# Last chain, weight loads and gate copies in another order, and sixteen spare products

## The chip, the cores and the metric

The kernel runs on one core of a Trainium2 chip. The metric is device time in microseconds of one execution, from start to end. Before the change it is 1464.82 us, the median of three runs (1464.5 to 1465.57).

## What is computed

Three layers follow one another: a global filter in the frequency domain, a soft mixture of experts, and a gated feed-forward layer.

```python
def _attn_ref(x, filt_r, filt_i):                 # x: 8 x 3072 x 256
    X = np.fft.rfft(x, axis=1)
    F = (filt_r + 1j * filt_i)[None, :, :]
    return np.fft.irfft(X * F, n=x.shape[1], axis=1)

def _moe_ref(x, phi, w1, w2):                     # 24576 tokens, 8 experts, 4 slots each
    logits = x @ phi
    d = np.exp(logits - logits.max(0, keepdims=True))
    d /= d.sum(0, keepdims=True) + 1e-09          # over all tokens
    slot_input = (d.T @ x).reshape(E, S_per_e, D)
    for e in range(E):
        h = np.maximum(slot_input[e] @ w1[e], 0.0)
        slot_out[e] = h @ w2[e]
    c = np.exp(logits - logits.max(1, keepdims=True))
    c /= c.sum(1, keepdims=True) + 1e-09          # over the 32 slots
    return c @ slot_out.reshape(n_slots, D)

def _moe2_ref(x, w_gate, w_val, w_out):           # 256 -> 1536 -> 256
    g = x @ w_gate
    return (g / (1.0 + np.exp(-g)) * (x @ w_val)) @ w_out
```

The third layer is applied to `c @ slot_out`, so `x @ w_gate` is `c @ (slot_out @ w_gate)`, a product over 32 slots only. The kernel uses that: it makes the small matrices `slot_out @ w_gate` and `slot_out @ w_val` once (the gates) and multiplies them by `c` for all tokens.

## The kernel before

The program is written in an order by hand (`manual_schedule`): each engine executes its instructions in the order in which the code issues them. Waits between engines come from the data and from memory that is used again. Tiles of closed pools give their memory to later tiles, and a later tile's first writer then waits for the last readers and writers of the earlier ones.

**Phase 1** takes the sequences through the transform in steps (`s1_chunk`, `s2_unit`, `tr_unit`), half a sequence at a time, six units a step. Behind each sequence `b` runs `chain(b, last)`, a generator of some dozen stages, most of them a group of small TensorE products and a copy to SBUF. It brings the sequence's logits back to the token domain, stores them (`lgd`), takes their maximum (`cm`, `mb`) and exponentials (`dd`), transforms these (`bd`, `dt`, `dh`) and multiplies them by the sequence's data, the `y` tiles (L482). The result `sl` is the sequence's part of the slots. `pump` advances the chains between the units. The chains of the last two sequences, `g6` and `g7` (chain 6 and the last chain), are interleaved by hand behind the last unit (L747 to L755). `combine` (L517) makes the weights by which the eight parts are added: `al` and `sm` on 32 partitions, spread to 128 by a product (`psb`, L536), and a product of each part with its weighted identity (`rb`), fourteen for the first seven parts (`pss`, L548) and two for the last (L502). The sum goes to `sp`.

**The transition** loads the second expert weights on SyncE's queue (`load_w2`, L770; the order of the loads is that of two loops), and the gate weights `wg` and `wv` (`flat_load`, L127). These tiles lie where phase 1's tiles lay, so some loads wait for phase 1's last products. It then runs the experts in two halves: `stage1` (`h`, L812), `turn` (transposes `t`, L829), `stage2` (`o`, L837; its first product reads `w2_0`). `later["first"]()` (L911) loads the first tile of mixing weights `c` from `cd` and the prepared output weights `wo`. Then come `so` and `sot`, the gate products (L872 and L883) and their split into a rounded part and a rest (`gh` and `gl`, in FP32R, each 128 x 512). Sixteen copies from SBUF to SBUF (L895) spread them over the partitions of `g4` and `v4`, eight on SyncE's queue and eight on GpSimd's. Columns 0 to 511 of the gates need no such copy.

**Phase 2** has 576 items of 512 tokens and 128 columns. For each, `gv` issues the products G and V (L988, L989), ScalarE takes the Silu (`s`, L991), VectorE multiplies (`h`, L997), `split` makes `hi` and `lo` (L1004, L1005), and `proj` issues six products `o` (L1026), three or four items behind `gv` (`lag`). In the first twelve items `load_out(i)` makes a rounded part and a rest of one chunk of `wo` on ScalarE (L977) and GpSimd (L978). The last group of twelve items is issued by `close` (L1048, L1052), with the copies and sums of its end (L1060, L1061) and four stores (L1069). The pool `kp` holds the tiles `s`, `h`, `hi`, `lo`, `ot` and `tmp`.

The order of the stages of phase 2's engines is one loop:

```python
        for i in range(len(items) + LAG):
            if i < len(items):
                ...
                gv(i)
            while todo and todo[0] <= i - lag(i):
                n = todo.pop(0)
                (close if n >= len(items) - NF else proj)(n)
            if i < len(items):
                gate(i)
            if i < NF:
                load_out(i)
            if 0 <= i - 1 < len(items):
                split(i - 1)
```

Of the kernel before, what the change touches and what calls it, by code (L numbers as in the profile page):

```python
# [20 lines left out]
NF = FF // 128  # L21
LAG = 4
EXP_AT = 17
HOLD = 9
# [55 lines left out]
def spectral_softmoe_glu_kernel(  # L80
# [56 lines left out]
    def phase1():  # L137
        with ExitStack() as c1:
# [4 lines left out]
            cvp = c1.enter_context(tc.tile_pool(name="cvp", bufs=1))  # L143
# [5 lines left out]
            ps_s1 = c1.enter_context(tc.tile_pool(name="ps_s1", bufs=1, space=PSUM))  # L149
            ps_x = c1.enter_context(tc.tile_pool(name="ps_x", bufs=2, space=PSUM))  # L150
            ps_t = c1.enter_context(tc.tile_pool(name="ps_t", bufs=1, space=PSUM))
            ps_l = c1.enter_context(tc.tile_pool(name="ps_l", bufs=1, space=PSUM))
            ps_c = c1.enter_context(tc.tile_pool(name="ps_c", bufs=1, space=PSUM))
# [154 lines left out]
            def chain(b, last):  # L308
# [3 lines left out]
                def two(late=False):  # L312
# [9 lines left out]
                    ps = ps_s1.tile([128, 1024], F32, tag="s1", name="cl")  # L322
                    return [ps[:, 0:512], ps[:, 512:1024]]

                def pair(name):
                    if b == NB - 2 and name in ("dt", "dh"):
                        t = ytp.tile([128, 768], F32, tag="yt", name=name)
                        return [t[:, 0:512], t[:, 512:768]]
# [58 lines left out]
                cm = chp.tile([128, E], F32, tag="cm", name="cm")  # L387
# [9 lines left out]
                both = bass.AP(pl[0].tensor, pl[0].offset, [list(pl[0].ap[0]), [16, E], [512, 2], [1, 16]])  # L397
                dve.tensor_reduce(out=cm, in_=both, axis=AX.XY, op=ALU.max)
                for h in range(2):
                    act.copy(lg[h], pl[h].rearrange("p (e n) -> p e n", n=16))  # L400
# [7 lines left out]
                if not last:  # L408
                    yield
                ps = small()  # L410
                pe.transpose(out=ps[0:32, 0:128], in_=cm, identity=ident)
                dve.tensor_reduce(
                    out=mb[:, b:b + 1],
                    in_=ps[0:32, 0:128].rearrange("p (g n) -> p g n", g=2)[:, :, 0:48],
# [22 lines left out]
                if last:  # L437
# [3 lines left out]
                bd = chp.tile([128, E, 32], F32, tag="lg", name="bd")  # L441
                pl = (ps_s1.tile([128, 1024], F32, tag="s1", name="cl") if last else small()).rearrange(
                    "p (g e n) -> p g e n", g=2, n=16
                )
                for h in range(2):
                    for g in range(2):
# [5 lines left out]
                        )  # L452
                for es in es2:
                    turn(bd, pl[:, :, es].rearrange("p g e n -> p e g n"), es)
                yield
                ps = two(True)
                for jj in range(NJ):
# [6 lines left out]
                    )  # L464
                dt_ = evac("dt", ps)
# [7 lines left out]
                for k in range(6):  # L473
                    pe.transpose(out=col(ps, k), in_=col(dt_, k), identity=ident)
                if last:
                    rb, pss = next(com)
                dh = evac("dh", ps)
                yield
                ps = two(True)[0] if b == NB - 2 else small()
                for k in range(6):  # L480
# [9 lines left out]
                    if k in (2, 5) and b == NB - 2:  # L490
                        yield
# [4 lines left out]
                act.copy(sl, ps[:, 0:256])  # L496
                if b < NB - 2:
                    nc.scalar.dma_start(out=sld[:, b, :], in_=sl)
                if last:
                    next(com)  # L500
                    for d_ in range(2):
                        pe.matmul(  # L502
                            out=pss[d_][:, 0:32], lhsT=sl[:, d_ * 128:(d_ + 1) * 128], rhs=rb[:, b, :],
                            start=False, stop=True,
                        )
                        (dve.tensor_copy if d_ else act.copy)(sp[:, d_, :], pss[d_][:, 0:32])
# [9 lines left out]

            def combine():  # L517
# [5 lines left out]
                beta4 = chp.tile([128, NB, 1], F32, tag="beta4", name="beta4")  # L523
                dve.tensor_reduce(out=mx, in_=mb, axis=AX.X, op=ALU.max)
                dve.tensor_scalar(al, mb, mx, None, ALU.subtract)
                act.activation(al, al, AF.Exp)
                yield
# [4 lines left out]
                dve.tensor_scalar(al, al, sm, 2.0 / SEQ, ALU.mult, ALU.mult)  # L532
                yield
                rb = chp.tile([128, NB, 32], F32, tag="t4", name="rb")
                psb = ps_t.tile([128, 512], F32, tag="T", name="psb")
                pe.matmul(out=psb[:, 0:NB], lhsT=rep4[0:32, :], rhs=al)  # L536
                dve.tensor_copy(beta4[:, :, 0], psb[:, 0:NB])
                dve.tensor_tensor(
                    out=rb,
                    in0=rep4[:, None, 0:32].to_broadcast([128, NB, 32]),  # L540
                    in1=beta4.to_broadcast([128, NB, 32]),
                    op=ALU.mult,
                )
                pss = [ps_x.tile([128, 512], F32, tag="X", name="pss") for _ in range(2)]
                yield rb, pss
                for d_ in range(2):
                    for b in range(NB - 1):
                        pe.matmul(  # L548
                            out=pss[d_][:, 0:32],
                            lhsT=slots[b // 4][:, b % 4, d_ * 128:(d_ + 1) * 128],  # L550
                            rhs=rb[:, b, :],
# [587 lines left out]
```

## Time and profile before

| what | us |
|---|---|
| median of three runs | 1464.82 (1464.5 to 1465.57) |
| the profiled execution | 1466.01 |
| its span in the trace | 1464.2 |
| phase 1 up to the last product of the last chain | about 378 |
| transition (experts, gates) up to the first output product | 378.7 to 410.8 |
| phase 2 | 410.8 to the end |
| busy: TensorE, VectorE, ScalarE, GpSimd | 1414.5, 1147.1, 905.0, 243.4 |

Times in the rows are counted from the start of the span. A span is 1.8 us shorter than its execution's own time. In phase 2 TensorE executes eight products an item without a pause; between chain 6 and the first output product the engines wait for one another, and this is the stretch that the rows below show closely.

### The profile page before, as it was taken

The numbers are of one execution on the slowest core, as the hardware profiler recorded it, in microseconds if no ns is written. First come the engines' busy times: TensorE is split into PE (matmuls) and PEld (weight loads), VectorE is DVE, ScalarE is ACT, GpSimd is POOL, SyncE is SP. The second block draws the span as 40 slices with busy tenths as digits, with TensorE's granted clock in tenths as the row PEclk, the third lists the DMA queues.
The fourth block names the chain that finished last, engine by engine and source line by source line (L and its number), as shares of the span: only waits on it lengthen the run. The fifth ranks groups of instructions, "written<-read, shape, count | busy, mean of one in ns | idle before, by whom it ended". The sixth has DMA issues, their size and how long they took to land.

```text
span 1464.2 us, 22633 instructions
## 1 busy us (share of the span) xinstructions
PE 1414.5 (97%) x8446; PEld 1101.4 (75%) x8446; DVE 1147.1 (78%) x1776; ACT 905.0 (62%) x1650; POOL 243.4 (17%) x315
## 2 busy tenths in 40 slices
PE   4899999998999999999999999999999999999998
PEld 2566666665567888888888888888888888888887
DVE  2788888877188878878887897888779878877775
ACT  2466667764266667666766666676666667666664
POOL 0466666663030000000000000000000000000000
PEclk9999999999999999999999999999999999999999
DMA  9979888978721231231131112212210320221111
GB/s 230 158 121 165 148 135 145 185 156 338 281 50 19 37 67 24 37 61 30 30 59 40 29 31 56 40 29 44 55 29 15 73 40 16 54 47 21 24 29 30
DMA packets 178077, 116.26 MB, mean 79 GB/s; under 512 B 105136, under 2 KB 161328, under 8 KB 177840
## 3 DMA queue, kind: packets, MB, share of 16 engines
q1 hardware_dynamic: 170720, 102.37, 35.6%
q10 hardware_dynamic: 6800, 11.54, 2.7%
q8 instruction: 67, 1.10, 0.3%
q0 software_dynamic: 448, 0.92, 0.2%
q14 instruction: 42, 0.34, 0.1%
HBM read 68.13 MB, written 34.60 MB: 70 GB/s over the span
## 4 chain that ended last, share of the span: by engine, by line
PE 91%; DVE 4%; ACT 2%; DMA 1%; issue 1%; POOL 1%; SPq 0%; ACTq 0%; POOLq 0%; DVEq 0%
PE o L1026 52%; PE V L989 9%; PE G L988 9%; PE X L258 5%; PE s L230 4%; PE T L283 2%; PE L L291 1%; PE c L482 1%; DMA x<-in_x_dram 1%; DVE sg L238 1%; PE o L1048 1%; PE c L364 1%; DVE P L262 1%; PE h L812 1%; PE c L447 1%
## 5 line engine op out<-in xcount | busy, mean ns | idle before, releaser
L1026 PE MATMUL o<-hi,wo 128*128 128x512 f32 x2256 | 696.3, 390 | 2.7 <-POOL wo L978 2.7
L991 ACT ACTIVATE s<-G 128x512 f32<-128x512 f32 x576 | 344.7, 598 | 331.7 <-PE G L988 327.6
L997 DVE TENSOR_TENSOR h<-V,s 128x512 f32<-128x512 f32 x576 | 393.5, 683 | 154.6 <-ACT s L991 151.8
L1026 PEld LDWEIGHTS o<-hi,wo 128*128 128x128 f32 x2256 | 424.5, 188 | 91.3 <-POOL wo L978 3.0
L1026 PE MATMUL o<-lo,wo 128*128 128x512 f32 x1128 | 439.5, 390 | 0.0
L1005 DVE TENSOR_TENSOR lo<-h,hi 128x512 fp32r<-128x512 f32 x576 | 421.5, 732 | 1.1
L1004 ACT CAST hi<-h 128x512 fp32r<-128x512 f32 x576 | 354.2, 615 | 36.4 <-DVE h L997 35.1
L1026 PEld LDWEIGHTS o<-lo,wo 128*128 128x128 f32 x1128 | 212.0, 188 | 43.9
L989 PE MATMUL V<-c,v 128*128 128x512 f32 x576 | 224.9, 390 | 1.2 <-DVE h L997 1.2
L988 PE MATMUL G<-c,g 128*128 128x512 f32 x576 | 224.7, 390 | 0.3 <-ACT s L991 0.3
L258 PEld LDWEIGHTS X<-fwd,b 128*128 128x128 f32 x768 | 95.2, 195 | 57.0 <-issue 40.3
L989 PEld LDWEIGHTS V<-c,v 128*128 128x128 f32 x576 | 108.4, 188 | 25.0 <-DVE h L997 2.7
L988 PEld LDWEIGHTS G<-c,g 128*128 128x128 f32 x576 | 108.2, 188 | 24.4 <-ACT s L991 1.1
L238 DVE STREAM_TRANSPOSE sg<-s 128x1024 f32<-128x1024 f32 x64 | 78.9, 1236 | 58.4 <-PE s L230 56.7
L258 PE MATMUL X<-fwd,b 128*128 128x128 f32 x768 | 111.6, 289 | 2.2 <-ACT b L247 1.2
L935 POOL TENSOR_TENSOR lg<-lg,mx 96x1024 f32<-96x1024 f32 x7 | 16.8, 2405 | 550.3 <-DVE mx L933 550.3
L230 PE MATMUL s<-x,csm 48*64 48x512 f32 x512 | 73.7, 632 | 18.6 <-DMA x<-in_x_dram 16.6
L247 ACT COPY b<-sg 128x768 f32<-128x768 f32 x64 | 59.0, 925 | 52.8 <-DVE sg L238 52.6
L271 POOL TENSOR_TENSOR yt<-P 128x256 f32<-128x256 f32 x96 | 70.4, 734 | 117.7 <-DVE P L262 117.2
L1031 DVE STREAM_TRANSPOSE ot<-o 128x512 f32<-128x512 f32 x94 | 65.1, 714 | 29.6 <-PE o L1026 29.6
L262 DVE TENSOR_TENSOR P<-X,ft 128x512 f32<-128x512 f32 x96 | 64.6, 672 | 12.0 <-PE X L258 11.8
L273 POOL TENSOR_TENSOR yt<-Q 128x256 f32<-128x256 f32 x95 | 69.5, 731 | 0.2
(202 smaller groups left out, 969.6 us busy)
## 6 DMA issues: line engine op xcount, KB each, us to landing
out_dram<-ot SPq DMA_DIRECT2D x192, 128.0 KB, 2.8
x<-in_x_dram SPq DMA_DIRECT2D x60, 384.0 KB, 8.2
w<-in_moe_w_dram SPq DMA_DIRECT2D x8, 1024.0 KB, 10.2
w<-in_moe_w_dram ACTq DMA_DIRECT2D x13, 512.0 KB, 6.9
c<-ch SPq DMA_DIRECT2D x42, 128.0 KB, 2.4
c<-cl SPq DMA_DIRECT2D x42, 128.0 KB, 2.4
raw<-in_moe_w_gate_dram SPq DMA_DIRECT2D x12, 256.0 KB, 5.2
raw<-in_moe_w_val_dram SPq DMA_DIRECT2D x12, 256.0 KB, 5.8
```

The source lines that it names most:

```text
L230: pe.matmul(out=ps[64 * k:64 * k + 64, 16 * r:16 * r + 16, :], lhsT=s1t_sb[64 * r:64 * r + 48, :], rhs=xt[step][64 * r:64 * r + 48, k, :, ...
L238: dve.transpose(out=sg.rearrange("p j d k -> p d j k"), in_=ps.rearrange("p n d -> p d n"))
L258: pe.matmul(out=ps[:, g].rearrange("p r m -> p (r m)"), lhsT=bb[:, j, :], rhs=fwd[:, j, :])
L262: dve.tensor_tensor(out=P, in0=ps, in1=f, op=ALU.mult)
L271: pool.tensor_tensor(out=y[:, :, 0, :], in0=P[:, :, 0, :], in1=P[:, :, 1, :], op=ALU.subtract)
L988: pe.matmul(out=pg, lhsT=g4[c][:, fs], rhs=c4[b][:, q, G, :])
L989: pe.matmul(out=pv, lhsT=v4[c][:, fs], rhs=c4[b][:, q, G, :])
L991: act.activation(s, pg, AF.Silu)
L997: dve.tensor_tensor(out=h, in0=pv, in1=s, op=ALU.mult)
L1004: act.copy(hi, h)
L1005: dve.tensor_tensor(out=lo, in0=h, in1=hi, op=ALU.subtract)
L1026: pe.matmul(out=a[h], lhsT=w[:, k, h], rhs=m, start=(f == 0 and n == 0), stop=(f == NF - 1 and n == 2), skip_group_check=True,)
```

## The change

1. **Weight loads of stage 1.** The `w1` loads are issued on SyncE's queue instead of ScalarE's, and earlier. Pools are placed so that this is possible (`cvp` on the other side, a new pool `w6`, PSUM pools in another order); three `pump(1)` fewer than ten remain, so chain 6's `dd` product comes later.
2. **The last chain.** The maximum `cm` is made in two reductions between the two copies `lg`. Chain 6's L482 products are split into pieces of eight, four, four and eight between products of the last chain. In `combine` the weights are spread before the sum of exponentials is known, VectorE adds up the parts in a running sum (`acc`) and multiplies by the last weight in `sl`; the fourteen `pss` products are gone, and the factor `sm` comes with `rb`. Seven products of 128 columns without a use (`warm`) stand in the chain.
3. **Second expert weights.** The loads come in another order, and `w2_0` lies elsewhere in SBUF (it was the first tile of the stack, and is now behind `gl`), by which all tiles between lie 8 KB lower.
4. **Gates.** One subtraction of 64 partitions instead of two of 32, with another order of rows. The first three chunks of `wo` are split ahead of the cast of `gh`. Of the sixteen copies twelve go to SyncE's queue and four to GpSimd's.
5. **Phase 2.** Nine products without a use (`warm`) stand ahead of the first output products. The last two items are issued at the end, one accumulator after the other, and the output of the last group leaves in halves over three queues.

```diff
-            for g in (g6, g7, g6, g7, g7, g6, g7, g6, g6):
+            for n, g in enumerate((g6, g7, g6, g7, g7, g6, g6, g7, g6, g7, g6, g7, g6, g6, g7)):
                 next(g, None)
-            for _ in g7:
-                pass
+                if n == 2:
+                    warm(2)
...
-                act.copy(sl, ps[:, 0:256])
+                if last:
+                    warm(2)
+                    rb, beta4, acc = next(com)
+                    dve.scalar_tensor_tensor(sl, ps[:, 0:256], beta4[:, b:b + 1], acc, ALU.mult, ALU.add)
+                else:
+                    act.copy(sl, ps[:, 0:256])
...
+            def warm(n):
+
+                ps = ps_x.tile([128, 512], F32, tag="X", name="warm")
+                for _ in range(n):
+                    pe.matmul(out=ps[:, 0:128], lhsT=ident, rhs=ident)
...
-                for d_ in range(2):
-                    for b in range(NB - 1):
-                        pe.matmul(
-                            out=pss[d_][:, 0:32],
-                            lhsT=slots[b // 4][:, b % 4, d_ * 128:(d_ + 1) * 128],
-                            rhs=rb[:, b, :],
-                            start=(b == 0),
-                            stop=False,
-                        )
...
-        w2s[0] = one([128, 8, D], "w2_0")
-
...
         gh = one([128, 512], "gh", dt=F32R)
         gl = one([128, 512], "gl", dt=F32R)
-        one([128, 10 * D], "pad")
+        w2s[0] = one([128, 8, D], "w2_0")
+        one([128, 2 * D], "pad")
...
-        for e in (6, 7, 0):
+        for e in (6, 7):
             load_w2(e)
         flat_load(wg, wd[0], 128)
-        for e in (5, 4, 1, 2, 3):
+        for e in (5, 1, 4, 2, 3):
             load_w2(e)
         flat_load(wv, wd[1], 128)
+        load_w2(0)
...
-            for r in (32, 96):
-                dve.tensor_tensor(out=dst[r:r + 32, :], in0=pg[r:r + 32], in1=dst[r:r + 32, :], op=ALU.subtract)
+            dve.tensor_tensor(out=dst[64:128, :], in0=pg[64:128], in1=dst[64:128, :], op=ALU.subtract)
+        for f in range(EARLY):
+            later["load_out"](f)
...
-                (nc.sync if r < 2 else nc.gpsimd).dma_start(
+                (nc.sync if r % 2 or c == 2 else nc.gpsimd).dma_start(
                     out=later[n][c][32 * r:32 * r + 32, :].bitcast(F32),
-                    in_=(gl if r % 2 else gh)[32 * i:32 * i + 32, :].bitcast(F32),
+                    in_=(gl if r >= 2 else gh)[32 * i:32 * i + 32, :].bitcast(F32),
...
+                if 1 < i < 4:
+                    warm(3)
                 gv(i)
+                if i == 3:
+                    warm(3)
...
+        close([len(items) - 2, len(items) - 1])
```

On TensorE, from chain 6's last products to the experts' `h`, the order before is this (L482 of `cl` is chain 6, of `c` the last chain; `xN` is a row of N like instructions):

```order
L474 MATMUL cl<-csm,dt 128x128 x6
L411 MATMUL c<-csm,cm 32x128
L420 MATMUL c<-csm,mb 128x32
L482 MATMUL cl<-y,dh 32x256 x12
L447 MATMUL cl<-dd,csm 64x512 x4
L482 MATMUL cl<-y,dh 32x256 x12
L459 MATMUL cl<-fwd,bd 32x128 x24
L474 MATMUL cl<-csm,dta 128x128 x4
L474 MATMUL cl<-csm,dtb 128x128 x2
L536 MATMUL psb<-al,csm 128x8
L482 MATMUL c<-y,dha 32x256 x16
L482 MATMUL c<-y,dhb 32x256 x8
```

and after the change, where L495 is what L482 was:

```order
L495 MATMUL cl<-y,dh 32x256 x8
L456 MATMUL c<-dd,csm 64x512 x4
L551 MATMUL psb<-al,csm 128x8
L495 MATMUL cl<-y,dh 32x256 x4
L470 MATMUL cl<-fwd,bd 32x128 x24
L495 MATMUL cl<-y,dh 32x256 x4
L487 MATMUL cl<-csm,dta 128x128 x4
L487 MATMUL cl<-csm,dtb 128x128 x2
L572 MATMUL psn<-sm,csm 128x1
L495 MATMUL cl<-y,dh 32x256 x8
L495 MATMUL c<-y,dha 32x256 x16
L495 MATMUL c<-y,dhb 32x256 x8
```

The last eight products of chain 6 have moved behind the last chain's L459 and L474 products, and `psb` ahead of them.

On SyncE's queue, the loads of the second expert weights and of the gate weights, with buffer numbers, before:

```order
L770 DMA w2_6_4739<-in_moe_w2_dram 128x2x1024
L770 DMA w2_7_4743<-in_moe_w2_dram 128x2x1024
L770 DMA w2_0_4671<-in_moe_w2_dram 128x2x1024
L127 DMA wg_4755<-wgd_66 128x2x1536
L770 DMA w2_5_4735<-in_moe_w2_dram 128x2x1024
L770 DMA w2_4_4731<-in_moe_w2_dram 128x2x1024
L770 DMA w2_1_4683<-in_moe_w2_dram 128x2x1024
L770 DMA w2_2_4687<-in_moe_w2_dram 128x2x1024
L770 DMA w2_3_4691<-in_moe_w2_dram 128x2x1024
L127 DMA wv_4759<-wvd_67 128x2x1536
```

and after:

```order
L804 DMA w2_6_4758<-in_moe_w2_dram 128x2x1024
L804 DMA w2_7_4762<-in_moe_w2_dram 128x2x1024
L128 DMA wg_4774<-wgd_66 128x2x1536
L804 DMA w2_5_4754<-in_moe_w2_dram 128x2x1024
L804 DMA w2_1_4698<-in_moe_w2_dram 128x2x1024
L804 DMA w2_4_4750<-in_moe_w2_dram 128x2x1024
L804 DMA w2_2_4702<-in_moe_w2_dram 128x2x1024
L804 DMA w2_3_4706<-in_moe_w2_dram 128x2x1024
L128 DMA wv_4778<-wvd_67 128x2x1536
L804 DMA w2_0_4742<-in_moe_w2_dram 128x2x1024
```

`w2_0` went from the third place to the last. In the program of the change the load of `w2_1` waits for chain 6's last L495 product, and the load of `w2_0` for the last chain's last one.

On ScalarE, from the last gate cast into phase 2, with the semaphores that each instruction waits for (DMAHW are those of SyncE's and ScalarE's DMAs, DMASW those of GpSimd's), before:

```order
L875 CAST v4_0_4830<-h_4938 128x512 [waits PE_49]
L891 CAST gh_4719<-t_4944 128x512 [waits PE_49]
L991 ACTIVATE s_5011<-G_5007 128x512 [waits DMAHW2_49,DMAHW3_49,DMAHW1_49,PE_49]
L977 CAST wo0_4833<-wo0_4833 128x256 [waits DMAHW1_49]
L991 ACTIVATE s_5021<-G_5017 128x512 [waits PE_49]
```

and after, where L1026 is the Silu and L963 the cast of `wo`:

```order
L909 CAST v4_0_4850<-h_4957 128x512 [waits PE_49]
L963 CAST wo0_4853<-wo0_4853 128x256 [waits DMAHW1_49]
L963 CAST wo0_4853<-wo0_4853 128x256 x2
L926 CAST gh_4734<-t_4968 128x512 [waits PE_49]
L1026 ACTIVATE s_5036<-G_5032 128x512 [waits DMAHW2_49,DMAHW1_49,DMAHW4_49,DMAHW0_49,DMAHW5_49,DMASW6_49,DMAHW6_49,DMASW4_49,DMAHW7_49,DVE_49,PE_49]
L963 CAST wo0_4853<-wo0_4853 128x256
L1026 ACTIVATE s_5046<-G_5042 128x512 [waits PE_49]
```

The casts of three chunks stand ahead of `gh`, and the first Silu of phase 2 waits for more DMAs: on SyncE's queue, behind the cast of `gh`, stand now:

```order
L930 DMA g4_1_4848<-gh_4734 32x512
L930 DMA g4_1_4848<-gl_4738 32x512
L930 DMA v4_1_4851<-gh_4734 32x512
L930 DMA v4_1_4851<-gl_4738 32x512
L930 DMA g4_2_4849<-gh_4734 32x512 x2
L930 DMA g4_2_4849<-gl_4738 32x512 x2
L930 DMA v4_2_4852<-gh_4734 32x512 x2
L930 DMA v4_2_4852<-gl_4738 32x512 x2
```

Before, eight stood there, one for each pair of a target and a source.

## Rows read from the trace of the kernel before

**Rows 1.** The page: busy time of the engines, and the chain by engine.

```profile
PE 1414.5 (97%) x8446; PEld 1101.4 (75%) x8446; DVE 1147.1 (78%) x1776; ACT 905.0 (62%) x1650; POOL 243.4 (17%) x315
...
PE 91%; DVE 4%; ACT 2%; DMA 1%; issue 1%; POOL 1%; SPq 0%; ACTq 0%; POOLq 0%; DVEq 0%
```

**Rows 2.** Windows: length, busy us of PE, PEld, DVE, ACT, POOL, granted clock, DMA, GB/s.

```profile
361.40:368.40 7.00, 7.00 (x68) 2.87 (x63) 2.86 (x6) 1.01 (x3) 1.04 (x3) 0.51 0.77 313
368.40:378.70 10.30, 8.62 (x124) 6.80 (x118) 2.27 (x11) 2.20 (x6) 0.00 (x0) 1.00 0.95 376
378.70:382.00 3.30, 3.30 (x16) 0.84 (x20) 0.00 (x0) 0.00 (x0) 0.00 (x0) 0.50 1.03 410
...
410.80:416.20 5.40, 5.40 (x13) 4.24 (x14) 3.81 (x3) 1.41 (x3) 2.72 (x4) 0.50 0.48 123
```

**Rows 3.** The chain of waits in order of time: start us, us, what.

```profile
364.75 2.72 PE cl L482 x24
...
371.22 0.35 PE psb L536 x2
371.57 2.75 PE c L482 x48
374.32 3.24 PE pss L548 x28
...
378.67 7.03 PE h L812 x48
...
388.90 1.86 PE o L837 x32
```

**Rows 4.** Timeline of TensorE at 337 us: start, us, operation, [idle before, releaser].

```profile
337.56 0.65 PE L447 MATMUL c<-dd,csm 48*64 48x512 f32 x2 [1.10 <-DVE Q L263]
```

**Rows 5.** SyncE: its longest wait at L770 (us, times, longest), and the load `wv`.

```profile
SPq L770 <- PE cl L482: 13.6, 1, 13.6
...
L127 SPq DMA_DIRECT2D wv<-wvd x1: 443/443/443, 371.4 to 371.4; - x1
...
DMA to landing us min/median/max: 16.6/16.6/16.6
```

**Rows 6.** DMA issues between 300 and 420 us: count, KB each, median us to landing.

```profile
c<-cd ACTq DMA_DIRECT2D x2, 384.0 KB, 6.8
...
lgd<-lg SPq DMA_DIRECT2D x4, 96.0 KB, 2.3
lgd<-lg POOLq DMA_DIRECT2D x4, 96.0 KB, 5.9
```

**Rows 7.** The gate copies on SyncE (first and last of eight), and landing of all.

```profile
405.57 0.60 SPq L895 DMA_DIRECT2D g<-gh  x1
...
410.08 0.78 SPq L895 DMA_DIRECT2D v<-gl  x1
...
DMA to landing us min/median/max: 2.0/2.8/3.4
```

**Rows 8.** Timeline of ScalarE, VectorE and TensorE at the first items of phase 2.

```profile
404.96 0.59 ACT L891 CAST gh<-t 128x512 fp32r<-128x512 f32 x1 [1.30 <-PE t L883]
405.44 0.61 ACT L991 ACTIVATE s<-G 128x512 f32<-128x512 f32 x1
...
407.69 0.69 DVE L1005 TENSOR_TENSOR lo<-h,hi 128x512 fp32r<-128x512 f32 x1
...
410.79 1.22 PE L1026 MATMUL o<-hi,wo 128*128 128x512 f32 x2 [2.68 <-POOL wo L978]
```

**Rows 9.** The end: timeline, and landing of the last stores.

```profile
1458.23 1.46 DVE L1061 TENSOR_TENSOR ot<-o,tmp 128x256 f32<-128x256 f32 x4 [3.84 <-ACT tmp L1060]
...
1458.55 0.28 PE L1052 MATMUL o<-wo,lo 128*128 128x256 f32 x1
1459.73 1.73 SPq L1069 DMA_DIRECT2D out_dram<-ot  x4
...
DMA to landing us min/median/max: 1.9/2.2/2.3
```

More of the change, by code (lines that the diff above doesn't have):

```diff
@@ L452, in chain @@
                         )
+                if last:
+                    next(com)
                 for es in es2:
@@ L464, in chain @@
                     )
+                if last:
+                    next(com)
                 dt_ = evac("dt", ps)
@@ L489, in chain @@
                         )
[L490 removed]
+                    if k < 5 and b == NB - 2:
                         yield
@@ L924, in first, with load_out @@
                 )
+        def load_out(f):
+            st = wo[f][:, 1, :].bitcast(F32)
+            act.copy(wo[f][:, 0, :], st)
+            pool.tensor_tensor(out=wo[f][:, 1, :], in0=st, in1=wo[f][:, 0, :], op=ALU.subtract)
         def build(b):
@@ new lines, in part @@
+        def part(i, t):
+            f = items[i][3]
+            a = acc[0][t]
+            ts = slice(128 * t, 128 * t + 128)
+            pe.matmul(
+                out=a, lhsT=hhi[i][:, ts], rhs=wo[f].rearrange("p k d -> p (k d)"),
+                start=(f == 0), stop=(f == NF - 1), skip_group_check=True,
+            )
+            pe.matmul(
+                out=a[:, D:2 * D], lhsT=hlo[i][:, ts], rhs=wo[f][:, 0, :],
+                start=False, stop=(f == NF - 1), skip_group_check=True,
+            )
@@ new lines, in rows, with close @@
+        def rows(i):
+            accs(i)
+            for t in (2, 3, 0, 1):
+                part(i, t)
+            hhi.pop(i)
+            hlo.pop(i)
+        def close(two):
+            b, q, G, _ = items[two[0]]
+            row = b * SEQ + 1024 * q + 16 * G
+            ot = kp.tile([128, 4, D], F32, tag="ot", name="ot", bufs=2)
+            for t in range(4):
+                for i in two:
+                    part(i, t)
+                a = acc[0][t]
+                tmp = kp.tile([128, D], F32, tag="tmp", name="tmp", bufs=4)
+                act.copy(tmp, a[:, D:2 * D])
+                dve.tensor_tensor(
+                    out=ot[:, t].rearrange("p (m h) -> p h m", h=2),
+                    in0=a[:, 0:D].rearrange("p (h m) -> p h m", h=2),
+                    in1=tmp.rearrange("p (h m) -> p h m", h=2),
+                    op=ALU.add,
+                )
+                if t % 2:
+                    for ii in range(4):
+                        (nc.sync if ii % 2 == 0 else nc.scalar if t == 3 else nc.gpsimd).dma_start(
+                            out=bass.AP(out.tensor, (row + 4 * ii + t - 1) * D, [[32 * D, 32], [1, 2 * D]]),
+                            in_=ot[32 * ii:32 * ii + 32, t - 1:t + 1].rearrange("p t d -> p (t d)"),
+                        )
@@ L1079, in lag, with warm @@
             return min(LAG, 3 + i // 10)
-        todo = list(range(len(items)))
+        spare = ps_o.tile([128, 512], F32, tag="o3", name="spare")
+        def warm(n):
+            for _ in range(n):
+                pe.matmul(out=spare, lhsT=g4[0][:, 0:128], rhs=c4[0][:, 0, 0, :])
+        todo = list(range(len(items) - 2))
         gen = build(1)
```

183 lines of the change are left out of this document (88 added, 95 removed).

## The prediction, written before the changed kernel was run

> **What bounds the kernel now.** I began with the shares of the page [rows 1]. TensorE is busy for 97% of the span, and 91% of the chain of work that ended last is its own. Phase 2, nearly three quarters of the span, is the same on both sides of the change except for its first items and its last group, so it takes no part in the sum. What can move lies in the stretch from chain 6 to the first output products, and in the last five microseconds.
>
> For that stretch I read the windows [rows 2], then the chain of waits [rows 3]. The windows say where TensorE runs at its lower level. In three stretches of 7.0, 3.3 and 5.4 us the granted clock is 0.50 or 0.51, which is 1.2 of the 2.4 GHz, and TensorE is busy in all of each. Work done at half speed costs half of its time, so these stretches cost 3.5, 1.65 and 2.7 us. The last of them follows a pause of 2.68 us [rows 8].
>
> In the chain one product group follows the other: the last products of chain 6, the last chain, `pss`, then `h` (stage 1), `o` L837 (stage 2). Two things in it are not TensorE's. One is `c L447` of chain 6, which waits 1.10 us for VectorE at 336 us [rows 4]. The other is the gate section, where the first output product waits 2.68 us for GpSimd's `wo` [rows 8].
>
> Then I read the loads, since they stand beside the chain and the shares show nothing of them [rows 5]. SyncE's load of `w2` waits 13.6 us for the products of chain 6 (L482), which read memory that the weights reuse. This point, R, is 364.75 + 2.72 = 367.47 us. Behind R the same queue issues five loads of `w2` and `wv`. `wv`, the last of them, is issued at 371.4 and lands 16.6 us later, at 388.0. So **the last of 6.5 MB lands at R + 20.5 us**. Before, that is `wv`, which nothing needs before the gates.
>
> **Part 1: chain 6 and the last chain.** The products of chain 6 that waited for VectorE move behind other work: -1.0 us of the 1.10. The fourteen `pss` products, 3.24 us, go to VectorE as a running sum that is made while TensorE works. `psb`, 0.35 us, and the wait ahead of it, some 0.4, leave the path. The seven spare products of 128 columns fill pauses of TensorE; in their place the reduced `pss` pair and its copies stay. Taking these together, `h` starts 4.5 us earlier (bounds 3.5 and 7.3, the upper one with the half-clock stretch at `h` gone as well). By itself this brings stage 2 from 388.90 to 384.4. The `w1` loads move from ScalarE's queue to SyncE's and up to a dozen units earlier; no step of the chain [rows 3] waits for them before, and earlier they land no later, so they cost nothing, unless SyncE is held up at one of them, and then it holds up the `w2` loads too, which the next parts price. The reductions and copies that go from one engine to the other (`cm`, `y` of units 4 and 5) are worth tenths and stay within the bounds.
>
> **Part 2: what the new order does to R.** In the order of the change, chain 6's last eight products stand behind the last chain's L459 and L474 products, directly ahead of `c L482`. The products that must be done before `c L482` are the same ones as before, so R moves to about where that group begins: 371.57 - 1.0 - 0.75 = 369.8. With full clock in all of the stretch it is 368.4, with half clock kept in it 370.8; I take 369.5.
>
> **Part 3: the loads.** The program of the change issues `w2_1`, 4, 2, 3, `wv` and then `w2_0` behind R. These are again five loads of 1 MB and one of 1.5 MB, but now the last is `w2_0`, and stage 2's very first product reads it. It lands at 369.5 + 20.5 = 390.0 if nothing joins it. Something does: `first()` issues two loads of `c` on ScalarE's queue as soon as the last `h` is done, and that now falls into the wait. Stores issued by GpSimd beside a full SyncE queue took 5.9 us to land, the same stores from SyncE with the queue nearly empty 2.3 [rows 6], so two queues share what there is. The four loads of `c` landed within 6.8 us; half of them is at most 3.4 us ahead of `w2_0`. Bounds 0 and 3.4, I take the middle, 1.7. The Trainium skill says the same from its side ("DMA: Bandwidth & Descriptors", "Queues, rings and completion order": each engine takes turns between the queues that have work, packet by packet), which points to the upper bound and would add 1.7 us to the sum; a strict order of issue would take 1.7 from it. The trace's 5.9 against 2.3 is on the rule's side.
>
> So stage 2 begins at 391.7 instead of 388.90: **+2.8 us**, from 0.0 (R at 368.4, no sharing) to +5.8 (370.8, all of it). TensorE stands idle for some 7 us ahead of it, and behind the one long pause that the rows show the clock was at half. The three stretches cost 1.65, 2.7 and 3.5 us; I take 2.6, near that behind the pause: together **+5.4**, from +1.65 to +9.3. The 4.5 us of part 1 end in this wait and are worth nothing.
>
> **Part 4: gates and the first output products.** The copies of `gh` and `gl` go to SyncE twelve at a time instead of eight, GpSimd keeps four. The eight rows on SyncE stand 0.64 us apart, from 405.57 to 410.08, and land 2.0 to 3.4 us later, median 2.8 [rows 7]. Before, no engine waited for them at this point: the first `s` of phase 2 starts at 405.44, as the cast of `gh` ends [rows 8]. In the program of the change that first `s` names nine DMA semaphores instead of three, down to the copies of `gh` into `v4_2`, which are the ninth and the tenth on SyncE's queue; the order below the change shows it. The reason is memory: `gh` moved by 8 KB with `w2_0`, into what phase 2's pool `kp` covers. The tenth copy is issued 9 x 0.64 = 5.8 us behind the cast and has landed 2.8 us later, so `s` starts at the cast's end + 8.65 (ninth copy at 0.60 a step, landing 2.0: +6.8; tenth with landing 3.4: +9.3).
>
> From `s` to the end of the first `lo` it took 408.38 - 405.44 = 2.94 us. Ahead of the first output product now stand G and V of item 3 and three spare products of the same shape, which cost 0.4 at full and 1.3 at half clock; I take 0.8. The half clock that follows the pause begins with G of the third item, so only some 2.8 of its 5.4 us fall on output products: 1.4 (bounds 0 and 2.7). After: 8.65 + 2.94 + 0.8 + 1.4 = 13.8 behind the cast. Before: the first output product at 410.79 is 5.24 behind the cast, with 2.7 of half clock 7.94. **+5.9 us**, from +2.2 to +8.2. The earlier casts and subtractions of three chunks of `wo` and the one subtraction of 64 rows instead of two of 32 gain nothing now: the row of copies covers them. Without that cover the first output product would no longer wait for `wo`, which is the rival below. The nine spare products lie in the wait but for the three just counted.
>
> The Trainium skill speaks against this term ("DMA: Bandwidth & Descriptors", "Issuing engines are not separate DMA queues"): to start DMAs on several engines saves only the time to issue them, usually small beside the transfer. Here the ten issues, 5.8 us, are twice the landing; by the trace's rows the rule's "usually" doesn't hold for 64 KB copies.
>
> **Part 5: the end.** The last product ends at 1458.83, four additions end at 1459.69, and four issues on SyncE take 1.73 us before the last landing of 2.2 [rows 9]. With half of the output issued earlier and the rest on two queues, two issues of 0.43 fall away: **-0.9**, from -0.4 (one) to -1.3 (three).
>
> **Sum.** +5.4 + 5.9 - 0.9 = +10.4 us. Against the profiled execution (1466.01, its span 1464.2) this is 1476.4; against the median of three runs, 1464.82, it is **1475.2**. Of the bounds: +1.65 + 2.2 - 1.3 = +2.5 and +9.3 + 8.2 - 0.4 = +17.1, so 1467.3 to 1481.9.
>
> **Rivals.**
> *`s` doesn't wait for the copies* (the wait is real in the program, but the copies might land sooner than eight in a row did). Then the output products start at 2.94 + 0.8 + 1.4 = 5.15 behind the cast, -2.8 against before. 5.4 - 2.8 - 0.9 = +1.7: 1466.5, no change. Against it: the 0.64 us steps.
> *`w2_0` isn't late.* This is the other side: if fewer loads stand behind R, or R comes early enough, stage 2 starts when the chain lets it, -4.5 (down to -7.3). -4.5 + 5.9 - 0.9 = +0.5: 1465.3, and 1462.5 at the bound, not slower. It decides at `w2_0` landing before about 384.4. For it: a part of the 20.5 us may be what was still queued ahead of R before. Against it: 5 x 1024 + 1536 KB are 6.8 million bytes, at the rates of these windows (376 to 410 GB/s) [rows 2] 16.6 to 18.1 us by themselves, and R + 16.6 is 386.1.
> *Neither wait holds:* -4.5 - 2.8 - 0.9 = -8.2: 1456.6, faster.
> *Issues cost next to nothing*, so that `s` waits one landing alone, 2.8 us: 2.8 + 2.94 + 0.8 + 1.4 = 7.9, no different from before; 5.4 + 0.0 - 0.9 = +4.5: 1469.3. This is the skill's rule of part 4 taken at its word.
>
> **How the numbers follow.** The forecast gets 0.76, of which 0.02 end within 0.2% (2.93 us, about what a measurement of this kernel can tell from no change). The rival of cheap issues 0.05 (slower), `s` without a wait 0.08 (within), `w2_0` not late 0.07 (0.06 within, 0.01 faster), neither 0.04 (faster). So faster 0.05, within 0.16, slower 0.79. The range leaves out the last two rivals, the low edge of the second, and what lies above the forecast's nearly worst case: 1466.0 to 1481.0.
>
> **What would show it.** In the profile of the changed kernel: `pss` down to two products and `h` starting some 4 us earlier; the last load of `w2` issued behind L495 of chain 6 and landing some 22 us behind it; TensorE idle by about 7 us ahead of `o` L871 with "DMA" as what ended it; the first `s` of phase 2 some 8 us behind the cast of `gh`; half clock behind each of the two pauses; the last landing about 3.5 us behind the last product. If stage 2 starts before 386, or `s` within 3 us of the cast, the corresponding term is wrong and the kernel isn't slower by it.

## The result, and the profile after

The changed kernel takes 1480.05 us (median of four runs, 1478.69 to 1482.18), the kernel before beside it 1465.19 us: a ratio of 1.0106, with a 95% interval from 1.0091 to 1.0121. It is slower by 14.9 us. Forecast were 10.4 us and a range up to 1481.0. The profiled execution took 1479.66 us, its span is 1477.9, 13.7 us more than the span before, and in this span every microsecond can be placed.

TensorE's share of the chain that ended last fell from 91% [rows 1] to 87%, and DMA has 4% in place of 1%:

```profile
PE 87%; DVE 4%; DMA 4%; ACT 2%; issue 1%; POOL 1%; SPq 0%; ACTq 0%; POOLq 0%; DVEq 0%
```

The chain between 350 and 425 us, in order of time (start, us, what), answers to [rows 3]:

```profile
369.01 2.59 PE c L495 x48
371.60 0.20 PE warm L537
371.80 23.23 DMA w<-in_moe_w_dram
395.02 0.14 issue
395.16 3.64 PE o L871 x32
...
413.74 0.60 ACT gh L926
...
420.07 2.11 DMA v<-gh
...
422.43 0.61 ACT s L1026
```

The chain no longer runs through `pss` and the experts' `h`. It goes from the last chain's products straight to a DMA of 23.23 us, the load of `w2_0`, and from that to `o` L871. Further down it goes from the cast of `gh` through the SyncE queue's copies to the Silu, 422.43 - 414.33 = 8.1 us behind the cast. TensorE's longest waits in the same stretch (us, times, longest) say the same:

```profile
PE o L871 <- DMA w<-in_moe_w_dram: 12.8, 1, 12.8
PE G L1023 <- ACT s L1026: 7.0, 1, 7.0
```

Windows of the changed kernel (columns as in [rows 2]): the experts' `h`, the wait for `w2_0`, stage 2's first part, the gate wait, and the products behind it:

```profile
376.00:382.30 6.30, 6.30 (x56) 2.24 (x48) 1.28 (x2) 1.66 (x3) 0.00 (x0) 1.00 1.03 414
382.30:395.10 12.80, 0.03 (x1) 0.00 (x0) 0.75 (x2) 0.00 (x0) 0.00 (x0) 0.68 1.03 287
395.10:402.70 7.60, 7.54 (x74) 3.89 (x74) 0.00 (x0) 0.58 (x1) 0.00 (x0) 0.64 0.69 205
...
413.70:423.00 9.30, 2.06 (x7) 1.06 (x7) 0.69 (x1) 1.15 (x3) 3.19 (x6) 0.71 0.47 112
423.00:427.80 4.80, 4.72 (x10) 3.43 (x11) 4.20 (x7) 4.35 (x11) 2.68 (x4) 0.50 0.33 86
```

The last column but one is the share of the DMA engines: they are busy all through TensorE's pause of 12.8 us, but move 287 GB/s in it, against 414 in the window ahead. The 287 is a mean of three parts:

```profile
382.30:385.30 3.00, 0.03 (x1) 0.00 (x0) 0.75 (x2) 0.00 (x0) 0.00 (x0) 1.00 1.01 411
385.30:392.00 6.70, 0.00 (x0) 0.00 (x0) 0.00 (x0) 0.00 (x0) 0.00 (x0) 0.62 1.06 275
392.00:395.00 3.00, 0.00 (x0) 0.00 (x0) 0.00 (x0) 0.00 (x0) 0.00 (x0) 0.50 1.01 195
```

Behind each of the two pauses the granted clock is low, 0.64 (a mean over a stretch at half and one at full clock) and 0.50. The half clock at chain 6 and at `h` [rows 2] is gone: the `h` window stands at 1.00.

The gain is there too. In TensorE's timeline the experts' `h` begins at 373.76 instead of 378.67 [rows 3], and TensorE is done with it at 382.3. The table puts the steps beside one another:

| step | before | after | later by | of it, new in this step |
|---|---|---|---|---|
| `h` begins | 378.67 | 373.76 | -4.9 | -4.9 |
| stage 2's first product begins | 388.90 | 395.16 | +6.3 | +11.2 |
| stage 2 ends | 397.62 | 406.39 | +8.8 | +2.5 (half clock) |
| cast of `gh` ends | 405.55 | 414.33 | +8.8 | 0.0 |
| G of the seventh item begins | 418.43 | 432.88 | +14.45 | +5.7 |
| end of the span | 1464.2 | 1477.9 | +13.7 | -0.75 |

### The profile page after: what moved, and what is told of

It is laid out like the page before. It is cut to its first block, busy times and chain, and to the rows that moved or that the text cites. A ratio compares the mean times of both kernels' runs of the same rounds, so it can differ in the third digit from the quotient of the medians.

```text
span 1477.9 us, 22653 instructions
## 1 busy us (share of the span) xinstructions
PE 1413.2 (96%) x8444; PEld 1101.2 (75%) x8444; DVE 1145.6 (78%) x1781; ACT 905.9 (61%) x1651; POOL 242.2 (16%) x313
## 4 chain that ended last, share of the span: by engine, by line
PE 87%; DVE 4%; DMA 4%; ACT 2%; issue 1%; POOL 1%; SPq 0%; ACTq 0%; POOLq 0%; DVEq 0%
PE o L1061 51%; PE V L1024 9%; PE G L1023 9%; PE X L261 4%; PE s L233 4%; PE T L286 2%; DMA w<-in_moe_w_dram 2%; PE L L294 1%; PE c L495 1%; DMA x<-in_x_dram 1%; DVE sg L241 1%; PE o L1081 1%; DVE P L265 1%; PE o L871 1%; PE c L369 1%
## 5 line engine op out<-in xcount | busy, mean ns | idle before, releaser
L1026 ACT ACTIVATE s<-G 128x512 f32<-128x512 f32 x576 | 344.5, 598 | 337.8 <-PE G L1023 325.8
```

The lines of the kernel that those rows point to most:

```text
L1026: act.activation(s, pg, AF.Silu)
```

## Experiments

The first four took back one of the two waits of the changed kernel, a part of one, or both. All ratios are to the kernel before on the same chip; its own runs lay between 1461.3 and 1469.3 us.

**`e1_w0_before_wv`: the load of `w2_0` ahead of `wv`.**

```diff
         for e in (5, 1, 4, 2, 3):
             load_w2(e)
-        flat_load(wv, wd[1], 128)
         load_w2(0)
+        flat_load(wv, wd[1], 128)
```

> The changed kernel with one edit: the load of w2_0 is issued ahead of wv instead of behind it. Theory: stage 2 waits for w2_0 alone, and that is late because 4 MB and wv stand ahead of it on the queue. Then w2_0 lands as the fifth load behind R, at about 384.5 us instead of 395.0, TensorE's pause ahead of stage 2 shrinks from 12.8 us to 2 to 4 us, and the time falls by 10.5 us, by up to 13 if the half clock of stage 2 goes too: 1467 to 1469.5. Rival: the pause only hides a second wait (ht, another w2, the clock), so that stage 2 still starts near 390 and the time falls by less than 5 us.

Measured: 1469.6 us, ratio 1.0024 (1.0013 to 1.0036), 10.5 us below the changed kernel and 0.1 us above the expected 1467 to 1469.5. TensorE's waits of this kernel:

```profile
PE G L1023 <- ACT s L1026: 7.0, 1, 7.0
PE o L871 <- DMA w<-in_moe_w_dram: 3.9, 1, 3.9
```

The wait for `w2_0` is down from 12.8 to 3.9 us, and nothing took its place; the wait for the Silu is as long as it was. Stage 2's first 16 products still took 3.64 us in this profile, twice their time at full clock, so the clock was at half behind these 3.9 us too.

**`e2_c_on_sync`: all four loads of the first `c` tile on SyncE's queue, behind `w2_0`.**

```diff
             for r in range(4):
-                (nc.sync if r < 2 else nc.scalar).dma_start(
+                nc.sync.dma_start(
                     out=t[32 * r:32 * r + 32].rearrange("p q G n -> p q (G n)").bitcast(F32),
```

> The changed kernel with one edit: the two loads of the first c tile that ScalarE's queue issued go to SyncE's queue, behind w2_0. Theory: these two, on a queue of their own, took transfer time from wv and w2_0, which landed 26 us behind R instead of 20.5. Then w2_0 lands at 389.5 to 390 us, and the time falls by 5 to 5.5 us, to about 1474.5. Rival: w2_0 lands late for a reason of its own (its place in memory, the end of a long row of loads): no change, within 1 us.

Measured: 1474.53 us, ratio 1.0060 (1.0037 to 1.0084), 5.5 us below the changed kernel. The DMA's piece of the chain and TensorE's wait in this kernel:

```profile
370.21 19.14 DMA w<-in_moe_w_dram
```
```profile
PE o L871 <- DMA w<-in_moe_w_dram: 8.8, 1, 8.8
```

`w2_0` took 19.14 us from its issue instead of 23.23, and TensorE's wait is 4.0 us shorter. Chain 6's last product ended at 367.36 here, so the load landed 22.0 us behind it, not 26.0. What the two loads on ScalarE's queue had taken from `w2_0` is therefore 4.0 us. The rest of the excess over 20.5, 1.5 us, stays, so the expected landing was missed, although the time was hit: the median fell by 5.5 us, of which this execution shows the 4.0, and a chain whose R came 1.65 us earlier, ahead of the edit. The low rate behind `w2_0` is there without a second queue as well:

```profile
386.00:389.30 3.30, 0.00 (x0) 0.00 (x0) 0.00 (x0) 0.00 (x0) 0.00 (x0) 0.50 1.08 215
```

**`e3_tmp_own_pool`: the four `tmp` tiles in a pool of their own behind `kp`.** No address changes; only `kp` no longer reaches into `gh`.

```diff
         kp = p2.enter_context(tc.tile_pool(name="kp", bufs=3))
+        tp = p2.enter_context(tc.tile_pool(name="tp", bufs=4))
...
-                tmp = kp.tile([128, D], F32, tag="tmp", name="tmp", bufs=4)
+                tmp = tp.tile([128, D], F32, tag="tmp", name="tmp")
```

> The changed kernel with one edit: the four tmp tiles (used only at the very end) come from a pool of their own behind kp; no address changes. Theory: the first Silu waits for the copies of gh only because kp as a whole reaches into gh's memory, with the part that tmp takes. Then the Silu starts within 0.3 us of the cast's end instead of 8.1 us behind it, the first output product about 4 us behind the cast instead of 13.5, and the time falls by 7 to 10 us, to 1470 to 1473. Rival: the copies bound the start anyway (g4 and v4 of the items from 4 on, issued 0.63 us apart), and TensorE waits there instead: less than 4 us.

Measured: 1469.92 us, ratio 1.0031 (1.0020 to 1.0042), 10.1 us below the changed kernel. (The profiled execution is 5.6 us above this median, and its chain begins some 5 us later; only distances are read from it.) ScalarE's timeline:

```profile
419.21 0.59 ACT L926 CAST gh<-t 128x512 fp32r<-128x512 f32 x1 [0.39 <-PE t L918]
419.70 0.60 ACT L1027 ACTIVATE s<-G 128x512 f32<-128x512 f32 x1
```

The Silu follows the cast at once, as it did before the change [rows 8], and the first output product starts 423.66 - 419.80 = 3.9 us behind the cast, against 13.5 in the changed kernel and 5.2 before. Two lines that only say from which pool four tiles come, used a thousand microseconds later, are worth 10 us.

**`e4_both`: both edits.**

> The edits of e1 and e3 together. Theory: the two waits are one behind the other and independent, so the gains add: 10.5 to 13 and 7 to 10, that is 1457 to 1462.5, which is 2 to 8 us faster than the kernel before. Rival: with a shorter first wait the gates come into the time of wv and c on the queues and wait for these instead; then the sum falls short by 2 us or more.

Measured: 1460.35 us, ratio 0.9962 (0.9944 to 0.9980): faster than the kernel before, 19.7 us below the changed kernel where the single gains sum to 20.6. The gains add to within 0.9 us, less than the intervals, so no dependence of the two waits shows. Here the 3.5 us that are left of the wait for `w2_0` didn't cost the clock:

```profile
384.00:386.00 2.00, 1.73 (x32) 1.12 (x32) 0.00 (x0) 0.00 (x0) 0.00 (x0) 1.00 1.07 297
```

**`e8_w0_fourth`: behind R the order 1, 2, 3, 0, 4, `wv`**, on top of `e4_both`. Stage 2 uses `w2_4` only in its second half.

```diff
-        for e in (5, 1, 4, 2, 3):
+        for e in (5, 1, 2, 3, 0, 4):
             load_w2(e)
-        load_w2(0)
         flat_load(wv, wd[1], 128)
```

> The kernel of e4_both with the loads behind R in the order 1, 2, 3, 0, 4, wv. Theory: TensorE still waited 3.5 us for w2_0 in e4_both; one load of 1 MB less ahead of it is 2.55 us. Stage 2 starts at 381.7 to 382.3 instead of 384.3 (in that trace's time), and the time falls by 2 to 2.5 us against e4_both. w2_4, needed some 5 us later, still lands in time. Rival: the next wait is right behind it (w2_4 or wv, which then share the DMA engines with c), and less than 1 us is left of the gain.

Measured: 1456.76 us, ratio 0.9949 (0.9935 to 0.9962); the same kernel once more gave 1457.99 us and 0.9964 (0.9951 to 0.9977):

> The kernel of e8_w0_fourth once more, as the other side of the run that follows on the same chip: 1455 to 1459 us, granted clock 1.00 in all windows between 366 and 411 us.

The wait for `w2_0` is nearly gone, but another has grown, that for `gl`, from 0.3 us in `e4_both` to 1.2:

```profile
PE spare L1132 <- DVE gl L926: 1.2, 1, 1.2
PE c L456 <- DVE dd L445: 1.0, 1, 1.0
PE o L870 <- DMA w<-in_moe_w_dram: 0.8, 1, 0.8
```

Behind it stands ScalarE, whose casts of `wo` come ahead of the cast of `gh` and now wait for the loads of `wo`; in `e4_both` they began at 399.0 without a wait:

```profile
ACT wo L962 <- DMA wo<-wod: 1.3, 1, 1.3
```

The rival held in part, then, with `wo` as the next load instead of `w2_4` or `wv`. By the ratios, the step from `e4_both` is about 0.1% or less, with intervals that overlap; by the spans it is 1.5 us (1454.7 and 1453.2). The expected 2 to 2.5 us are therefore not shown, but the kernel's medians are 8.0 and 6.0 us below those of before (1464.75 and 1463.98), and the fastest here. The granted clock was 1.00 from 366 to 411 us, as expected.

**`e6_before_w0_last`: the kernel before with `w2_0` loaded last.**

```diff
-        for e in (6, 7, 0):
+        for e in (6, 7):
             load_w2(e)
         flat_load(wg, wd[0], 128)
         for e in (5, 4, 1, 2, 3):
             load_w2(e)
         flat_load(wv, wd[1], 128)
+        load_w2(0)
```

> The kernel before with one edit: w2_0 is loaded last, behind wv, as in the change. Theory: the place of the load by itself costs nothing where the chain is as long as before. w2_0 then lands where wv landed, R + 20.5 = 388.0 us, and stage 2 begins at 388.9 as now: within 1 us of before. The loss of the change comes from the load's place together with the loads of c that start earlier on ScalarE's queue, as the experts' h ends earlier. Rival: the late place costs by itself; then stage 2 starts 2 us or more later and the time rises by 2 to 5 us.

Measured: 1469.73 us (one of its eight runs, at 3636 us, is an outlier that the median passes over), ratio 1.0034 (1.0023 to 1.0046): 5.0 us slower. The size is that of the rival, a cost of the place by itself:

```profile
PE o L838 <- DMA w<-in_moe_w_dram: 3.0, 1, 3.0
```
```profile
371.18 18.79 DMA w<-in_moe_w_dram
...
390.10 3.50 PE o L838 x32
```

The reason is in the expectation's own count. In this kernel `w2_5` and the four others still stand behind R, so `w2_0` makes the sixth load of 1 MB, and the last byte lands not at R + 20.5 but one load later: R was 364.83 + 1.48 = 366.31, the landing 389.97, 23.7 behind it. In the changed kernel `w2_5` has moved ahead of R, which keeps the sum at 6.5 MB. Stage 2 began 3.0 us late and then ran its first 16 products in 3.50 us at half clock. So a last place behind 7.5 MB costs time with the old chain too. For the order of the change, with 6.5 MB behind R, this run decides nothing: by its figures `w2_0` would have landed at 366.31 + 20.5 = 386.8 (an estimate), and stage 2 was ready at 390.10 - 3.0 = 387.1. Whether that order would cost anything with the old chain isn't shown.

**`e7_copies_8_8`: the gate copies eight and eight, those that read `gh` on SyncE**, in the changed kernel.

```diff
-                (nc.sync if r % 2 or c == 2 else nc.gpsimd).dma_start(
+                (nc.sync if r < 2 else nc.gpsimd).dma_start(
```

> The changed kernel with the sixteen gate copies divided eight and eight between SyncE and GpSimd; the eight on SyncE are the eight that read gh. Theory: the first Silu waits for the last copy that reads gh, and what sets its time is the row of issues, 0.64 us each. The last is now the eighth instead of the tenth, so the Silu starts 6.6 to 6.9 us behind the cast's end instead of 8.1. Rival: the Silu waits for a fixed time or for all sixteen; then 8 us again, or 7.5 and more with the GpSimd ones last.

Measured in a single run: 1478.97 us, and in ScalarE's timeline and the chain:

```profile
421.45 0.60 ACT L1026 ACTIVATE s<-G 128x512 f32<-128x512 f32 x1 [7.93 <-DMA v<-gh]
```
```profile
418.08 2.99 DMA v<-gh
```

The cast ended at 412.94 + 0.59 = 413.53, so the Silu starts 7.9 us behind it, hardly sooner than 8.1. The issue was earlier as expected: the last copy that reads `gh` is issued 418.08 - 413.53 = 4.55 us behind the cast instead of 420.07 - 414.33 = 5.74. But it takes 2.99 us to land instead of 2.11, with eight of GpSimd's copies under way beside it. That GpSimd's copies are the reason is read from this one run and not tested. The row of issues is thus one part of the 8 us and the landing the other, and this division wins little as long as the Silu waits for the copies of `gh`. The rival, a wait for all sixteen, isn't excluded by this run, but by the changed kernel, where the last two copies of `gl` were issued 1.4 us and less ahead of the Silu (422.43), too late to have landed by then, since the shortest landing of a copy of `gl` took 1.9 us:

```profile
421.01 1.15 SPq L930 DMA_DIRECT2D v<-gl  x2
```

**`e5_no_spare` and `e10_e8_no_spare`: without the sixteen spare products**, in `e4_both` and in `e8_w0_fourth`.

```diff
-                if n == 2:
-                    warm(2)
...
-                    warm(2)
...
-                    warm(3)
...
-                if 1 < i < 4:
-                    warm(3)
...
-                if i == 3:
-                    warm(3)
```

> The kernel of e4_both without its sixteen products without a use (seven in the last chain, nine ahead of the first output products). Theory: these keep TensorE's clock up. In e4_both the granted clock is 1.00 from 361 to 410 us, in the kernel before 0.50 or 0.51 in three stretches there; without the spare products the half clock comes back at the experts' h (1.65 us before) and at the first output products (2.7 us before), so the time rises by 1.5 to 4.5 us against e4_both. Rival: the shorter waits alone keep the clock up, and then the time stays within 0.7 us of e4_both.

Measured: 1461.14 us, ratio 0.9976 (0.9964 to 0.9988), 0.8 us above `e4_both` by the medians and 0.14%, 2 us, by the ratios, which are to different runs of before; the intervals overlap, and this pair alone decides nothing. The granted clock at `h` (375 to 383) and at the first output products (404 to 411) is 1.00 without the spare products; 0.57 stands only behind the wait for `w2_0`, here 4.2 us:

```profile
375.00:383.00 8.00, 8.00 (x72) 2.74 (x64) 1.28 (x2) 1.78 (x3) 0.00 (x0) 1.00 1.03 414
383.00:387.00 4.00, 0.02 (x1) 0.00 (x0) 0.75 (x2) 0.00 (x0) 0.00 (x0) 1.00 1.04 387
387.00:391.00 4.00, 3.75 (x34) 1.86 (x35) 0.00 (x0) 0.00 (x0) 0.00 (x0) 0.57 1.03 294
...
404.00:411.00 7.00, 5.89 (x28) 2.85 (x18) 5.69 (x9) 6.55 (x16) 6.92 (x10) 1.00 0.43 103
```

> The kernel of e8_w0_fourth without its sixteen products without a use. In e5_no_spare the granted clock stayed at 1.00 at the experts' h and at the first output products although the sixteen were gone; half clock came only behind a wait of 4.2 us for w2_0, which this kernel doesn't have. Theory: the short waits keep the clock up and the sixteen products do nothing; within 1 us of e9_e8_again, the first output products at the same distance from the cast. Rival: they do hold the clock where a pause of some 1 to 2 us is left (ahead of h, ahead of the first output products); then a window at 0.50 to 0.75 shows there and the time is 1.5 to 4 us longer.

Measured: 1458.03 us, ratio 0.9960 (0.9946 to 0.9975), beside 1457.99 and 0.9964 for the same kernel with them, in the same runs of before: no difference, though each interval leaves 2 us to either side. The one profiled execution, the slowest of the six (1461.49 us), however, shows low clock in two windows, where the profile of `e9_e8_again` has 1.00:

```profile
366.00:371.00 5.00, 5.00 (x69) 3.38 (x70) 2.65 (x9) 0.78 (x2) 0.00 (x0) 0.57 0.28 109
...
404.00:411.00 7.00, 4.60 (x12) 2.87 (x12) 5.14 (x8) 6.22 (x15) 6.29 (x10) 0.78 0.54 136
```

So the first theory, that they hold the clock, isn't borne out by the times, and its opposite isn't borne out by every trace. Low clock in the first of these windows comes with all sixteen in place too, in `e3_tmp_own_pool`:

```profile
364.10:370.90 6.80, 6.80 (x70) 3.93 (x74) 2.95 (x9) 0.80 (x2) 0.00 (x0) 0.50 0.89 361
```

In the changed kernel itself they didn't help behind the two long pauses of 12.8 and 7.0 us: half clock followed both.

## Why the prediction was right, point by point

The time lies 0.95 us inside the upper edge of the range. Direction and both waits were right; the first wait was put too small.

**Parts 1 and 2, the chain and R.** `h` begins 4.9 us earlier (4.5 said). That the two agree is partly chance, since the pieces were others. The wait of 1.10 us in chain 6 is gone, but this brought nothing by itself: before and after, TensorE waits for VectorE a little later and goes on at the same time.

```profile
349.57 0.64 PE L291 MATMUL L<-yt,phi_sb 128*32 128x256 f32 x8 [1.34 <-DVE lts L303]
```
```profile
349.51 0.64 PE L294 MATMUL L<-yt,phi_sb 128*32 128x256 f32 x8 [1.34 <-DVE lts L306]
```

From there to the last chain's L482 (L495 after) the change gains 2.5 us, in a stretch that was at half clock for 7.0 us before [rows 2] and isn't now; from there to `h`, where `psb` and `pss` stood, 2.35 us. As `h` ran at full clock too, TensorE was ready for stage 2 6.6 us earlier (382.3 against 388.90), near the upper bound of 7.3. Chain 6's last product ended where `c L495` begins, 369.01 (R, 369.5 said, with 368.4 for full clock). That the gain of the chain is worth nothing behind the load held: TensorE was done with `h` at 382.3 and stood still for 12.8 us.

**Part 3, the loads.** The mechanism held, the size did not, and this is the term that was too small. `w2_0` landed at 371.80 + 23.23 = 395.0, that is R + 26.0; the forecast was 391.7, R + 22.2. `e2_c_on_sync` splits the excess of 5.5 us over R + 20.5: 4.0 us are the share of the two `c` loads on ScalarE's queue, put at 1.7 as the middle between 0 and 3.4, and 1.5 us are missing in the base, which is R + 22.0 without them.

The 4.0 us lie above even the upper end, which took half of what the four loads had needed. The price of these loads isn't their bytes at the rate of the weights: where they run nearly alone, the DMA engines are busy throughout and move 195 GB/s (392 to 395 us) and 215 GB/s (in `e2_c_on_sync`). At these rates 0.79 million bytes take 3.7 to 4.0 us, an estimate that fits the 4.0. Why they are slow no run tests; each of them writes 32 partitions, a load of weights 128. The Trainium skill's rule of turns between queues ("DMA: Bandwidth & Descriptors", "Queues, rings and completion order") was on the right side, and the trace agrees with it: from 385.3 to 392.0 SyncE's queue (q1) and ScalarE's (q10) both move packets (packets, MB, share), and moving the two loads behind `w2_0` in its own queue gave 4.0 us back.

```profile
q1 hardware_dynamic: 276, 1.07, 62.1%
q10 hardware_dynamic: 219, 0.77, 43.4%
```

It should have had the whole weight rather than half.

Where the other 1.5 us lie the traces do show. A load of weights ends with sixteen packets of 4 bytes. In `e2_c_on_sync` fifteen of those of `w2_0` stand by R + 18.5, as fourteen of those of `wv` did before (R + 18.6); the landing, with the last of them, comes at R + 22.0 and came at R + 20.5. So one late part of sixteen makes the difference. In both traces a part begins to fall behind at a load of 16 KB of instructions, which takes 1.1 to 1.4 us; whether that is the cause no run tests.

**The half clock behind the pause** cost 11.23 us for stage 2 instead of 8.72, 2.5 us; 2.6 was said. That choice among three sizes came out here, but it isn't the same in every kernel: stage 2's first 16 products took 1.8 us more than at full clock in `e1_w0_before_wv` and `e2_c_on_sync`, and none more in `e4_both`.

**Part 4, the gates.** The Silu started 8.1 us behind the cast (8.65 said), the first output product 13.5 us behind it (12.4 said, as 8.65 + 2.94 + 0.8), and with the clock the whole step cost 5.7 us where 5.9 was said. Two small errors cancelled: the copies were issued in steps of 0.63 and landed in 2.1, but between the Silu and the first output product stand two pairs of G and V and six spare products, where the forecast had counted one pair and three, and all of them ran at half clock. The output products from 427.81 on ran at full clock, so the 1.4 us of half clock forecast for them fell away. That the Silu waits because of the place of `gh` under `kp` is shown by `e3_tmp_own_pool`, where no address and no copy changed.

The rule of the Trainium skill on issuing engines ("DMA: Bandwidth & Descriptors", "Issuing engines are not separate DMA queues"), by which the time to issue is usually small beside the transfer, holds for one copy (0.63 us beside 2.1 of landing) and misleads for a row of ten: 5.7 us of issues stand beside 2.1 of landing. In `e7_copies_8_8` what was saved at the issue was mostly lost at the landing; that section says that DMAs of different issuers interleave on the same 16 engines, and the trace agrees as far as both queues ran at that time.

**Part 5, the end.** From the end of the last product to the last landing it was 4.4 us before and is 3.4 now: 1473.30 to 1476.7, with these last issues and landings:

```profile
1473.02 0.28 PE L1085 MATMUL o<-wo,lo 128*128 128x256 f32 x1
...
1474.20 0.85 ACTq L1115 DMA_DIRECT2D out_dram<-ot  x2
```
```profile
DMA to landing us min/median/max: 1.6/2.1/2.2
```

The gain between the seventh item and the end of the span is 0.75 us; 0.9 was said.

**The sum** of these, +6.3 + 2.5 + 5.7 - 0.75 = 13.7 us, is the difference of the two spans; the forecast's terms were +2.8 + 2.6 + 5.9 - 0.9. Nearly the whole miss of 3.3 us is in the first. The medians are 1.2 us further apart than the spans, which is no more than single executions differ.

**The rivals.** None held. The prediction says that its range leaves out the last two of them; the last, issues that cost next to nothing, at 1469.3, lies inside it. `e1` and `e3` show what two of them would have given: 1469.6 without most of the wait for `w2_0` (1465.3 was worked out) and 1469.9 without the wait of the Silu (1466.5). Neither wait held would have been faster than before, as `e4_both` shows, 1460.35; 1456.6 was worked out.

## What to carry to other kernels

A chain that was shortened is worth nothing until the next thing that it meets is ready: before making it shorter, put beside it the landing of each load that its next stage reads, and order the loads by first use, the first product's operand first. A pool that reaches into memory of earlier tiles makes its first writer wait for all of their readers, DMAs among them, even if the overlapping tile is used at the very end; the list of semaphores at that first instruction shows it, and putting the tile into a pool of its own removes it. Loads that start earlier because the work ahead got faster (those of `c` on ScalarE's queue at 381.7 instead of 388.3 us) are themselves a cost, if they share the DMA engines with the load that is waited for.

## What was unexpected of the hardware

Two `c` loads of 384 KB, 0.79 million bytes, on another queue delayed a load of 1 MB by 4.0 us, as much as 1.7 million bytes at the 414 GB/s of the window before; the rate during their transfer was 275 GB/s, and such loads nearly alone had 195 to 215. A load landed up to 3 us behind fifteen of its sixteen parts. The clock behind a pause was not the same each time: after a wait of 3.5 us in `e4_both` stage 2's first products ran at full clock (1.93 us for sixteen), after 3.9 and 4.2 us in `e1` and `e5` at half (3.64 and 3.53 us), and after 3.0 us in `e6` at half as well (3.50 us). The length of the pause alone doesn't decide it in these runs.
